# Batch 0's x in four loads in place of two, and the first states' cast ahead of alpha's turn

## The chip, the cores and the metric

The kernel runs on one core of one Trainium2 chip. The metric is the device time of one execution in microseconds. A core has five engines that run side by side, each through its own list of instructions: TensorE (PE in the profile, with its weight loads as PEld), VectorE (DVE), ScalarE (ACT), GpSimd (POOL) and SyncE (SP). Loads and stores are issued by an engine as instructions of its list, and move on the core's 16 DMA engines.

## The reference

Cross attention between 512 tokens and 32 states per head, both ways, and then a two-layer block on the rows that come out, with a PReLU between the layers:

```python
B, H, S, Ns, D = (8, 8, 512, 32, 64)
scores = scale * np.matmul(x, state.transpose(0, 1, 3, 2))
a = softmax(scores)                      # over the 32 states
xread = np.matmul(a, state)
scores2 = scale * np.matmul(state, x.transpose(0, 1, 3, 2))
a2 = softmax(scores2)                    # over the 512 tokens
sread = np.matmul(a2, x)
rows = np.concatenate([xread, sread], axis=2)   # heads side by side: [B * 544, 512]
h = rows @ w_in                          # d_ff = 2048
g = np.maximum(h, 0.0) + alpha * np.minimum(h, 0.0)
return g @ w_out
```

(The softmaxes are written out in the reference; the names here stand for them.)

## The kernel before

Everything is computed in f16 with f32 sums. The program is a long list of tokens, `ORDER`, and a table `steps` that gives the function for each token. The loop at its end calls them one after another, and each call appends its instructions to the lists of the engines. No scheduler moves anything: the order of the tokens is the order on every engine. A token `xt.0.1.0.3` is a call of the step `xt` with the arguments 0, 1, 0, 3; a letter at the end of some tokens names the engine that does a copy (a is ScalarE, v is VectorE, p is GpSimd).

The work goes by batches 0 to 7. For each, x is loaded and transposed, the scores of tokens against states are built, and the two softmaxes follow. The states are multiplied with w_in first (`m`, copied out by `mo`), so that the hidden layer of a batch is a product of softmax weights with these (`F` and `f`), followed by the PReLU (`N` on ScalarE, `G` on VectorE) and the second layer (`S`, `P`).

The steps around the change are all in the first lines of `ORDER`:

- `lx0` (`load_x0`) loads batch 0's x into the tile `xg_0` in two pieces: the even heads, then the odd ones. It is issued by GpSimd and turns f32 into f16 on the way. All the loads of x, `w_in` (`wi`, four pieces), `w_out` (`wo`) and the later states (`lst`) are issued by GpSimd too. The first 512 state rows (tile `st0_32`) are loaded by SyncE and alpha (`al32`) by ScalarE, ahead of the list.
- `id` builds the identity on GpSimd, which every transpose on TensorE needs as an operand. `ni` makes a negative identity from it on VectorE.
- `oma` turns alpha into 1 - alpha on VectorE (four 32x32 transposes and one operation). The PReLU reads it.
- `stc` casts the first states to f16 on VectorE. `stt` transposes them on TensorE (eight matmuls), `sto` copies them out on ScalarE.
- `Z.7.n` issues products of zeros on TensorE, n blocks of 128 columns in instructions of up to 512; nobody reads the result.
- `xt.b.j.g` transposes four heads of one parity g of batch b (j is one half of the tokens). `xo` copies them out. For batch 0 the even heads come first.
- `lx.1` loads batch 1's x in one piece, and `xt.1...` transposes it on TensorE.

Transfers that GpSimd issues signal on eight semaphores in turn. The ninth load takes the first's again, so it waits until that load has landed.

The program's list begins:

```python
lx0.0 lx0.1 id ni.v wi.0 oma lst stc Z.7.32 stt.2 sto.a lx.1 wi.1 dd.0.0.v wi.2 Z.7.3 xt.0.0.0.6
xo.0.0.0.v xt.0.1.0.3 xo.0.1.0.v Z.7.10 xt.0.0.1.4 xt.0.1.1.0 xo.0.1.1.v dd.0.1.a sd.0.0.5 hm.0.0
```

Of the kernel before, what the change touches and what calls it, by code (L numbers as in the profile page):

```python
# [14 lines left out]


ORDER = """
lx0.0 lx0.1 id ni.v wi.0 oma lst stc Z.7.32 stt.2 sto.a lx.1 wi.1 dd.0.0.v wi.2 Z.7.3 xt.0.0.0.6
xo.0.0.0.v xt.0.1.0.3 xo.0.1.0.v Z.7.10 xt.0.0.1.4 xt.0.1.1.0 xo.0.1.1.v dd.0.1.a sd.0.0.5 hm.0.0
xo.0.0.1.a sd.0.1.6 hm.0.1 sc.0.2.1.2 tm.0 hs.0.0 he.0.0 ssum.0.0 wi.3 Z.3.2 hs.0.1 he.0.1 ssum.0.1  # L20
m.1.0.7.4 mo.1.0.a.1.0 m.0.0.3.0 mo.0.0.a.1.1 tms.0 mo.0.0.a.0 str.0.5 sro.0.a str.1.6 sro.1.v
# [118 lines left out]
def kernel(  # L140
# [56 lines left out]
    xgs = {}  # L197
# [16 lines left out]
    nc.scalar.dma_start(al32[:n_jc, :], moe_alpha.rearrange("(jc p) -> jc p", p=128))  # L214
    xgs[0] = att.tile([128, H, 2, 2, D], F16, name="xg_0", tag="xg", bufs=4)

    def load_x0(g):
        nc.gpsimd.dma_start(  # L218
            xgs[0][:, g::2].rearrange("p k j r d -> p k (j r d)"),
            x[0, g::2].rearrange("k (p j r) d -> p k (j r d)", j=2, r=2),  # L220
        )

    osb_all = consts.tile([128, 4, d_model], F32)
# [583 lines left out]
    def product_sum(b, i, n):  # L807
# [16 lines left out]
        "m": state_w_in, "mo": state_w_in_out,  # L824
        "F": first, "f": first_part, "Z": zeros, "N": negative, "G": prelu, "S": second, "O": second_out,
        "st": stored, "lx0": load_x0, "lf": load_x0_32, "cx": x0_cast, "id": identity,
        "L": second_piece, "LO": second_piece_out, "Ls": second_piece_stored,
        "W": weight_sum, "A": hidden_sum, "P": product, "C": product_out, "D": product_sum,
# [34 lines left out]
```

## Time and profile before

| what | value |
|---|---|
| runs of the kernel | 207.89, 208.69, 210.45 us; median 208.69 |
| profiled execution | 207.22 us |
| its span, first to last instruction | 205.4 us |
| granted TensorE clock | 1.00 throughout |
| HBM read, written | 17.31 MB, 8.91 MB |
| DMA queue of GpSimd's loads | 12704 packets, 8.59 MB |

The span is what the trace shows; 1.82 us of the profiled execution lie outside it. In the lines of the profile, L218 is line 218 of the kernel, `out<-in` are tiles by the program's names, x16 is a count of instructions, and what stands behind `<-` in brackets is what ended the engine's idle time ahead of the row. PE times overlap from one matmul to the next, since matmuls are pipelined. A DMA issue on POOL's list has the time that POOL spends on it; the landing is a time of its own.

### The profile page before, as it was taken

The numbers are of one execution on the slowest core, as the hardware profiler recorded it, in microseconds if no ns is written. First come the engines' busy times: TensorE is split into PE (matmuls) and PEld (weight loads), VectorE is DVE, ScalarE is ACT, GpSimd is POOL, SyncE is SP. The second block draws the span as 40 slices with busy tenths as digits, with TensorE's granted clock in tenths as the row PEclk, the third lists the DMA queues.
The fourth block names the chain that finished last, engine by engine and source line by source line (L and its number), as shares of the span: only waits on it lengthen the run. The fifth ranks groups of instructions, "written<-read, shape, count | busy, mean of one in ns | idle before, by whom it ended". The sixth has DMA issues, their size and how long they took to land.

```text
span 205.4 us, 5181 instructions
## 1 busy us (share of the span) xinstructions
PE 197.1 (96%) x2023; PEld 131.4 (64%) x2023; DVE 181.6 (88%) x321; ACT 145.2 (71%) x319; POOL 159.6 (78%) x136
## 2 busy tenths in 40 slices
PE   7887999999999999999999999999999999999993
PEld 2542344445757766766557776776778777788882
DVE  4799999999999989999899999989999699995841
ACT  2599997889897679899898878869666476411120
POOL 7575489999989979998998899987997988502220
PEclk9999999999999999999999999999999999999999
DMA  5999999995999342749990135022000220031124
GB/s 81 195 203 209 204 206 197 185 232 54 163 163 178 66 153 58 100 103 158 194 163 3 53 123 135 3 105 102 0 0 3 111 93 3 2 131 62 69 102 156
DMA packets 39257, 23.22 MB, mean 113 GB/s; under 512 B 22320, under 2 KB 35008, under 8 KB 39232
## 3 DMA queue, kind: packets, MB, share of 16 engines
q0 software_dynamic: 12704, 8.59, 29.3%
q1 hardware_dynamic: 26496, 14.29, 28.4%
q8 instruction: 16, 0.26, 0.6%
q14 instruction: 9, 0.07, 0.2%
q10 hardware_dynamic: 32, 0.01, 0.0%
HBM read 17.31 MB, written 8.91 MB: 128 GB/s over the span
## 4 chain that ended last, share of the span: by engine, by line
PE 85%; DVE 5%; DMA 5%; POOL 1%; ACT 1%; issue 1%; ACTq 0%; POOLq 0%
PE ps L793 44%; PE ps L620 24%; PE ps L675 7%; DMA xg<-in_x_dram 5%; PE ps L629 3%; PE ps L590 3%; DVE gt_all L656 3%; PE ps L553 1%; ACT neg_all L652 1%; PE ps L362 1%; DVE m_all L603 1%; POOL xg L218 1%; DVE ts L466 1%; DVE nb L514 1%; DVE mx L476 1%
## 5 line engine op out<-in xcount | busy, mean ns | idle before, releaser
L656 DVE SCALAR_TENSOR_TENSOR gt_all<-neg_all,oma_sb,ps 128x512 f16<-128x512 f32 x128 | 89.3, 738 | 3.0 <-ACT neg_all L652 2.7
L652 ACT ACTIVATE neg_all<-ps 128x512 f32<-128x512 f32 (+1 forms) x144 | 77.4, 598 | 20.0 <-PE ps L620 14.4
L620 PE MATMUL ps<-aT,m_all 128*128 128x512 f16 x250 | 66.4, 379 | 0.3 <-DVE m_all L603 0.2
L765 POOL TENSOR_TENSOR hc_all<-gt_all 128x512 f16<-128x512 f16 x43 | 49.2, 1160 | 11.4 <-DVE osb_all L810 8.7
L793 PEld LDWEIGHTS <-hc_all 128*128 128x128 f16 x480 | 46.3, 98 | 14.3 <-issue 1.1
L793 PE MATMUL ps<-wc,hc_all 128*128 128x256 f16 x360 | 47.7, 273 | 0.0
L793 PEld LDWEIGHTS <-gt_all 128*128 128x128 f16 x336 | 32.6, 98 | 8.3 <-issue 0.5
L805 ACT COPY osb_all<-ps 128x256 f32<-128x256 f32 x51 | 19.1, 383 | 25.7 <-PE ps L793 22.2
L620 PEld LDWEIGHTS <-m_all 128*128 128x128 f16 x250 | 24.0, 98 | 18.0 <-issue 2.2
L603 ACT CAST m_all<-ps 128x512 f16<-128x512 f32 x58 | 31.6, 621 | 4.3 <-PE ps L590 4.3
L765 POOL TENSOR_TENSOR hc_all<-gt_all,hc_all 128x512 f16<-128x512 f16 x22 | 25.4, 1164 | 6.3 <-DVE hc_all L765 6.1
L793 PE MATMUL ps<-w_out_sb,gt_all 128*128 128x256 f16 x224 | 29.7, 273 | 0.0
L765 POOL TENSOR_TENSOR hc_all<-hc_all,gt_all 128x512 f16<-128x512 f16 x21 | 24.3, 1164 | 3.9 <-DVE hc_all L765 3.6
L810 DVE TENSOR_TENSOR osb_all<-osb_all,ps 128x256 f32<-128x256 f32 x45 | 18.0, 413 | 7.6 <-PE ps L793 4.7
L496 POOL TENSOR_TENSOR an<-ts,r 128x1024 f16<-128x1024 f32 (+1 forms) x9 | 15.5, 1725 | 6.2 <-DVE r L493 4.0
L482 POOL TENSOR_TENSOR ts<-ts,mx 128x1024 f32<-128x1024 f32 x7 | 13.4, 1918 | 5.4 <-DVE mx L476 5.4
L675 PE MATMUL ps<-w_out_sb,gt_all 128*128 128x512 f16 x64 | 16.6, 380 | 0.1
L793 PE MATMUL ps<-w_out_sb,hc_all 128*128 128x256 f16 x120 | 16.5, 273 | 0.0
L793 PE MATMUL ps<-wc,gt_all 128*128 128x256 f16 x112 | 14.7, 273 | 0.0
L590 PE MATMUL ps<-w_in_sb,stT 64*32 64x512 f16 x256 | 11.8, 383 | 1.9 <-DMA w_in_sb<-in_moe_w_in_dram 0.9
L527 ACT ACTIVATE e<-ps,nb 128x512 f16<-128x512 f32 x16 | 11.1, 705 | 0.1
L675 PEld LDWEIGHTS <-gt_all 128*128 128x128 f16 x64 | 5.9, 98 | 7.2 <-issue 1.2
(78 smaller groups left out, 204.6 us busy)
## 6 DMA issues: line engine op xcount, KB each, us to landing
out_dram<-osb_all SPq DMA_DIRECT2D x33, 256.0 KB, 2.6
xg<-in_x_dram POOLq DMA_DIRECT2D x7, 512.0 KB, 9.1
w_in_sb<-in_moe_w_in_dram POOLq DMA_DIRECT2D x4, 512.0 KB, 12.0
w_out_sb<-in_moe_w_out_dram POOLq DMA_DIRECT2D x4, 512.0 KB, 13.6
xg<-in_x_dram POOLq DMA_DIRECT2D x2, 256.0 KB, 4.5
out_dram<-osb_all SPq DMA_DIRECT2D x2, 128.0 KB, 2.4
gs_all<-in_state_dram POOLq DMA_DIRECT2D x1, 192.0 KB, 6.8
st<-in_state_dram SPq DMA_DIRECT2D x1, 128.0 KB, 2.4
```

The source lines that it names most:

```text
L482: engine(e).tensor_tensor(ts, ts, over_blocks(cols(softmax_tile("mx", b), j, S // N)), ALU.subtract)
L496: engine(e).tensor_tensor(blocks(cols(softmax_tile("an", b), j, S)), blocks(cols(softmax_tile("ts", b), j, S)), over_blocks(cols(softmax_t ...
L590: nc.tensor.matmul(banks[N * k : N * (k + 1), (k0, k1)[g], :], st_head(b, 2 * k + g)[64 * g : 64 * g + 64, :], w_in_sb[64 * g : 64 * g + 6 ...
L603: copier(e)(ms[b, f][:, g, :], banks[:, live["mp", b, f][g], :])
L620: nc.tensor.matmul(h.rearrange("p (r t) -> p r t", r=2), ms[b, f][:, g, 128 * j : 128 * (j + 1)], weights(b, g), start=(g == 0), stop=(g = ...
L652: nc.scalar.activation(neg, h, RELU, bias=0.0, scale=-1.0)
L656: nc.vector.scalar_tensor_tensor(gts[b, f][:, j, :], negs.pop((b, jc)), oma_sb[:, jc : jc + 1], hs.pop((b, jc)), ALU.mult, ALU.add,)
L675: nc.tensor.matmul(outs[b, q], hidden(b, jc, q), w_out_sb[:, jc, :], start=(jc == 0), stop=(jc == n_jc - 1),)
L765: engine(e).tensor_tensor(t, x, y, ALU.add if s == 1 else ALU.subtract)
L793: nc.tensor.matmul(outs[b, i, bank], rows, cols, start=(p in (1, 2, 5) and jc == 0), stop=(jc == n_jc // 2 - 1), skip_group_check=True,)
L805: copier(e)(rows_at(b, q, k)[:, 256 * half : 256 * (half + 1)], outs[b, i, "x"])
L810: nc.vector.tensor_tensor(to, to, outs[b, i, bank], ALU.add)
```

## The change

Batch 0's x comes in four loads of two heads each: heads 0 and 2, 4 and 6, 1 and 3, 5 and 7. The first states' cast moves from behind alpha's step to just behind the identity's token, ahead of the negative identity and of alpha. The first zero products are 28 blocks (seven instructions of 512 columns) in place of 32 (eight).

```diff
-lx0.0 lx0.1 id ni.v wi.0 oma lst stc Z.7.32 stt.2 sto.a lx.1 wi.1 dd.0.0.v wi.2 Z.7.3 xt.0.0.0.6
+lx0.0.0 lx0.0.1 lx0.1.0 lx0.1.1 id stc ni.v wi.0 oma lst Z.7.28 stt.2 sto.a lx.1 wi.1 dd.0.0.v wi.2 Z.7.3 xt.0.0.0.6
...
-    def load_x0(g):
+    def load_x0(g, i):
+        pair = slice(4 * i + g, 4 * i + g + 3, 2)
         nc.gpsimd.dma_start(
-            xgs[0][:, g::2].rearrange("p k j r d -> p k (j r d)"),
-            x[0, g::2].rearrange("k (p j r) d -> p k (j r d)", j=2, r=2),
+            xgs[0][:, pair].rearrange("p k j r d -> p k (j r d)"),
+            x[0, pair].rearrange("k (p j r) d -> p k (j r d)", j=2, r=2),
         )
```

On GpSimd, the start of the list, before the change (xg_75 is batch 0's x, xg_124 batch 1's, gs_all holds the later states, DMASW0 to 7 are the eight semaphores of its loads):

```order
L218 DMA xg_75<-in_x_dram 128x4x256 x2
masks.py:197 MEMSET ident 128x128
masks.py:199 ISA
masks.py:199 AFFINE_SELECT ident<-ident 128x128 [waits Pool_49]
L253 DMA w_in_sb<-in_moe_w_in_dram 128x4x512
L247 DMA gs_all<-in_state_dram 128x768
L201 DMA xg_124<-in_x_dram 128x8x256
L253 DMA w_in_sb<-in_moe_w_in_dram 128x4x512 x3
```

And the same place now, where lines from 218 on stand one further down and batch 1's x is xg_125:

```order
L219 DMA xg_75<-in_x_dram 128x2x256 x4
masks.py:197 MEMSET ident 128x128
masks.py:199 ISA
masks.py:199 AFFINE_SELECT ident<-ident 128x128 [waits Pool_49]
L254 DMA w_in_sb<-in_moe_w_in_dram 128x4x512
L248 DMA gs_all<-in_state_dram 128x768
L201 DMA xg_125<-in_x_dram 128x8x256
L254 DMA w_in_sb<-in_moe_w_in_dram 128x4x512
L254 DMA w_in_sb<-in_moe_w_in_dram 128x4x512 [waits DMASW0_49]
L254 DMA w_in_sb<-in_moe_w_in_dram 128x4x512 [waits DMASW1_49]
```

Four issues stand ahead of the identity in place of two, and the third and fourth piece of w_in wait for the first and the second load of x. Each w_out piece, and each later batch of x, waits for the same load as before, by another semaphore, save the first two w_out pieces, which wait for the third and the fourth load of x.

On VectorE, the start of the list, before (al_72 is alpha, st_32_70 the first states in f32, gs_all holds their f16 copy and the negative identity):

```order
L394 MEMSET gs_all 128x256 x2
L384 TENSOR_SCALAR gs_all<-ident 128x128 [waits Pool_49]
L305 STREAM_TRANSPOSE alT<-al_72 32x32 [waits DMAHW1_49,DVE_49]
L305 STREAM_TRANSPOSE alT<-al_72 32x32 x3
L306 TENSOR_SCALAR oma_sb<-alT 128x16 [waits DVE_49]
L292 CAST gs_all<-st_32_70 128x256 [waits DMAHW0_49]
L398 COPY gs_all<-ps 64x8x32 [waits Activation_49]
```

And now:

```order
L395 MEMSET gs_all 128x256 x2
L293 CAST gs_all<-st_32_70 128x256 [waits DMAHW0_49]
L385 TENSOR_SCALAR gs_all<-ident 128x128 [waits Pool_49]
L306 STREAM_TRANSPOSE alT<-al_72 32x32 [waits DMAHW1_49,DVE_49]
L306 STREAM_TRANSPOSE alT<-al_72 32x32 x3
L307 TENSOR_SCALAR oma_sb<-alT 128x16 [waits DVE_49]
L399 COPY gs_all<-ps 64x8x32 [waits Activation_49]
```

The cast of the first states stands ahead of the operation that waits for GpSimd's identity, and waits only for its own load; alpha's five instructions stand behind both. On TensorE one zero product is gone ahead of the first states' transposes, and within the transposes of the even heads the first two now wait for the first load and the third for the second; the odd heads' wait for the third and the fourth load in the same way. ScalarE's and SyncE's lists are unchanged.

## The prediction

> **What bounds the kernel now.** I read the page's busy shares first, then the busy time by stretch, to see where the busiest engine is not busy.
>
> ```profile
> PE 197.1 (96%) x2023; PEld 131.4 (64%) x2023; DVE 181.6 (88%) x321; ACT 145.2 (71%) x319; POOL 159.6 (78%) x136
> ```
> ```profile
> 0.00:25.00 25.00, 20.45 (x283) 8.95 (x284) 20.08 (x40) 17.81 (x39) 15.36 (x23) 1.00 1.14 178
> 25.00:200.00 175.00, 174.75 (x1733) 120.99 (x1726) 160.63 (x281) 127.01 (x281) 144.24 (x114) 1.00 0.51 103
> ```
>
> The columns of the second view are the stretch and its length, then busy time of PE, PEld, DVE, ACT and POOL, the granted clock, the DMA share and GB/s. From 25 to 200 us TensorE is idle for 0.25 us; in the first 25 us it is idle for 4.55 us, and the DMA engines move 178 GB/s. The change edits only the program's first steps. So it can act in one way: by how much earlier or later TensorE's unbroken work begins. The ceiling is a few microseconds of 207.22.
>
> The chain of waits in order of time says what sets that beginning.
>
> ```profile
> 1.25 0.47 POOL xg L218
> 3.52 0.71 POOL w_in_sb L253
> 4.23 0.53 POOL gs_all L247
> 4.76 9.53 DMA xg<-in_x_dram
> 14.29 0.05 issue
> 14.34 1.07 PE ps L340 x16
> 15.41 0.45 PE ps L641 x2
> 25.12 1.89 PE ps L675 x8
> ```
>
> (Start, length, what; rows between some of these are left out.) One DMA, the load of batch 1's x, holds 9.53 us of the head. It is issued at 4.76 and lands at 14.29, and batch 1's sixteen transposes start at 14.34. Nothing on the chain before it is arithmetic; it is POOL issuing loads in order. The question is therefore what the change does to that landing, and what would be late next if it came sooner.
>
> **The loads on POOL's queue.** POOL issues every load of the head in order, and its identity lies between them:
>
> ```profile
> 1.25 1.69 POOL L218 DMA_DIRECT2D xg<-in_x_dram  x2 [0.80 <-POOLq L847]
> 3.22 0.29 POOL masks.py:199 TENSOR_SCALAR_AFFINE_SELECT ident<-ident 128x128 f16<-128x128 f16 x1
> 3.46 0.77 POOL L253 DMA_DIRECT2D w_in_sb<-in_moe_w_in_dram  x1
> 4.23 0.55 POOL L247 DMA_DIRECT2D gs_all<-in_state_dram  x1
> 4.76 0.91 POOL L201 DMA_DIRECT2D xg<-in_x_dram  x1
> 5.65 2.26 POOL L253 DMA_DIRECT2D w_in_sb<-in_moe_w_in_dram  x3
> ```
> ```profile
> L218 POOL DMA_DIRECT2D xg<-in_x_dram x2: 748/844/941, 1.2 to 2.2; - x2
> DMA to landing us min/median/max: 4.3/4.5/4.7
> ```
>
> The state load has 128 rows and takes 0.55 us to issue, a load of four heads (128x4 rows) 0.75 when it is not the first (the minimum above), a whole batch (128x8 rows) 0.91. The trace has no load of 256 rows. On the line between 128 and 512 rows it costs 0.55 + 0.20 x 128/384 = 0.62. The first load of all took 0.94, so 0.19 more; I keep that once. Now: 0.94 + 0.75 = 1.69. After: 4 x 0.62 + 0.19 = 2.67, which is **0.98 us more on POOL**. The bounds are four at the state load's price, 2.39 (0.70 more), and four at 0.75, 3.19 (1.50 more). I take 0.98, since the rows lie on both sides of it.
>
> Everything behind moves by that: the identity from 3.51 (3.22 + 0.29) to 4.49, the issue of w_in's first piece from 3.46 to 4.44, the states, batch 1's x to 5.74. Two of the later w_in issues now wait for the first and the second of the four loads; those land before 5.6 (below) and the issues come after 7, so these waits cost nothing.
>
> **Does a later issue mean a later landing?** Only if the queue runs dry. The DMA rates of the head:
>
> ```profile
> 3.00:3.25 0.25, 0.25 (x2) 0.15 (x1) 0.00 (x0) 0.00 (x0) 0.17 (x2) 1.00 0.44 10
> 3.25:3.50 0.25, 0.25 (x2) 0.07 (x1) 0.00 (x0) 0.00 (x0) 0.25 (x2) 1.00 0.03 4
> 3.50:3.75 0.25, 0.25 (x2) 0.08 (x1) 0.20 (x2) 0.00 (x0) 0.25 (x2) 1.00 0.39 39
> 3.75:4.00 0.25, 0.25 (x2) 0.14 (x1) 0.24 (x2) 0.00 (x0) 0.25 (x1) 1.00 1.23 150
> 4.00:5.00 1.00, 0.95 (x5) 0.04 (x5) 0.85 (x5) 0.00 (x0) 1.00 (x3) 1.00 1.44 196
> 5.00:6.00 1.00, 1.00 (x16) 0.83 (x17) 0.00 (x0) 0.41 (x1) 1.00 (x2) 1.00 1.46 197
> ```
>
> The last number is GB/s. Few bytes move before 3.5; the stream then holds 196 to 197. Batch 0's x is 2 x 256 KB (524,000 bytes written). Up to 6.00 the rows give 0.25 x (39 + 150) + 196 + 197 = 440,000, so the rest is through at about 6.43. The whole head is this one stream: batch 1's x lands when everything queued before it has gone through. Two things can move it.
>
> Its start: the first issue ends at 1.25 + 0.94 = 2.19 now, and at 1.25 + 0.62 + 0.19 = 2.06 after, so **0.13 us earlier**. The bounds are nothing (the stream starts by something else), and 0.25 earlier if it hangs on the second issue's end (2.94 now, 2.68 after).
>
> Its supply: w_in's issue ends at 4.23 now and at 5.21 after. The first load's bytes were seen from 3.00 on, 0.81 us after its issue ended, and the full stream from about 3.76 (the point from which 196 GB/s would give the same bytes), 1.57 after. With 0.81, w_in is ready at 6.02 and batch 0's x is through at 6.43 - 0.13 = 6.30: no gap. With 1.57 it is ready at 6.78: a gap of 0.48. I take no gap, because the slow stretch between 3.0 and 3.5 is that of an idle queue, and this queue is not idle; but the margin is 0.28 us, so the gap stays as a rival.
>
> A fixed price of each further load in the stream: the two loads are issued at 1.25 and 2.18 (1.25 + 0.94) and land 4.3 and 4.7 us later, at 5.55 and 6.88. That is 1.33 apart, which is 262,000 bytes at 197 GB/s. So I take nothing. [...]
>
> **The first states and the zero product.** TensorE's and VectorE's rows:
>
> ```profile
> 1.32 3.60 PE L272 MATMUL ps<-gs_all 128*128 128x512 f16 x8 [1.32 <-DVE gs_all L266]
> 2.15 0.15 PEld L272 LDWEIGHTS <-gs_all 128*128 128x128 f16 x1 [0.28 <-issue]
> 2.58 0.15 PEld L272 LDWEIGHTS <-gs_all 128*128 128x128 f16 x1 [0.28 <-issue]
> 4.96 0.58 PE L286 MATMUL ps<-ident,gs_all 128*64 128x128 f16 x8
> 5.65 0.61 PE L340 MATMUL ps<-ident,xg 128*128 128x128 f16 x8
> 6.93 0.62 PE L340 MATMUL ps<-ident,xg 128*128 128x128 f16 x8
> 15.24 0.59 PE L641 MATMUL ps<-aT,m_all 128*128 128x512 f16 x2
> ```
> ```profile
> 1.27 0.55 DVE L394 MEMSET gs_all<- 128x256 uint32 x2
> 3.66 0.84 DVE L305 STREAM_TRANSPOSE alT<-al 32x32 f32<-32x32 f32 x4
> 4.62 0.29 DVE L292 CAST gs_all<-st 128x256 f16<-128x256 f32 x1
> 13.45 1.30 DVE L504 STREAM_TRANSPOSE aT<-an 128x512 f16<-128x512 f16 x2
> 16.51 1.41 DVE L656 SCALAR_TENSOR_TENSOR gt_all<-neg_all,oma_sb,ps 128x512 f16<-128x512 f32 x2 [0.15 <-ACT neg_all L652]
> ```
>
> Eight zero products of 0.43 us (2.15 to 2.58) end at 4.92, the cast at 4.91, and the first states' transposes start at 4.96. With seven products TensorE is free at 4.49; the cast, moved ahead of alpha, is done well before; the identity comes at 4.49. So they start at about 4.54, 0.42 earlier (at POOL's upper bound, identity at 5.01, 0.10 later). That 0.42 has no buyer: the transposes of x behind them would start at 5.23 in place of 5.65, but their second load lands at 5.55 - 0.13 = 5.42. They wait. The same holds for the second half, which starts at 6.93 because its load lands at 6.88: now two of its transposes run on the third load, and six remain when the fourth lands at 6.75, so batch 0 is some 0.25 us earlier there. That too is hidden: batch 0's weights are ready at 14.75 (13.45 + 1.30) and their second product runs at about 15.45, so this branch already has 0.7 us to spare against batch 1's x. Alpha moves later by about 1 us, and its first reader is at 16.51.
>
> The cast now falls beside POOL's fourth issue. POOL's first issue, beside VectorE's fill of 0.55 us, took 0.94; the second, beside nothing, 0.75. [...] The row against it is batch 1's issue at 4.76, which ran beside the end of the cast at 4.62 and took 0.91, the least that any of the seven whole-batch issues took:
>
> ```profile
> L201 POOL DMA_DIRECT2D xg<-in_x_dram x7: 914/922/944, 4.8 to 90.0; - x7
> ```
>
> I take nothing for it.
>
> **The sum.** Batch 1's x lands at 14.29 - 0.13 = 14.16, w_in's pieces in the same stream move alike, and the end moves with them: 207.22 - 0.13 = 207.09 by the profiled execution, whose span of 205.4 leaves 1.82 outside. The runs shown are 207.89, 208.69 and 210.45; with the profiled one the middle of the four is 208.29, and less 0.13 that is **208.2**.
>
> **Rivals.**
>
> - *The stream runs dry ahead of w_in* (slower). It decides from the point where the four issues take over 0.28 us more than I sum, or where bytes follow an issue as late as they did the first, 1.57 us. Price: a gap of 0.48 less 0.13, so 0.35 later; at the upper bound of POOL's cost 0.52 more, 0.87. Time 208.6 to 209.2. For it: the margin is small. Against: the queue is not idle. Chance 0.27.
> - *The slow start shrinks* (faster). If the 0.5 us of few bytes (3.0 to 3.5) depends on the first load's size, the stream starts up to 0.5 earlier; w_in's issue then comes late and takes some of it back. Gain 0.4: 207.9. Chance 0.12.
> - *TensorE's clock rises later*. Its products cost 0.43 us per 512 columns at first a quarter of that, 0.11, per 128; eight of batch 0's x transposes then take 0.61 where that rate would make at least 0.86, so a faster rate arrives before 5.65. A pause after seven products could put it off; batch 0's branch would lose about 1 us of products, less its 0.7 to spare and the 0.25 gained: 0 to 0.3 later. Chance 0.06.
> - *Each load pays alone in the stream*. A load's landing comes 4.3 us after its issue starts, of which 1.33 is bytes: 3.0 us each, two more loads, 214.1. The 1.33 between two landings speaks against it. Chance 0.02.
>
> **Chances and range.** The forecast itself, from 0.25 earlier to 0.2 later, has 0.51; 0.02 is left on either side for what I don't see. About 2%, or 4.2 us, is what a measurement of this kernel can tell from no change. Only the single-payment case and what is left reach beyond it: faster 0.02, slower 0.04, within 0.94. The range is the rivals' ends set on the runs' scatter: from 207.22 - 0.4 = 206.8 to 208.69 + 0.87 = 209.6.
>
> **What would show it.** Right: POOL's four issues take about 2.7 us, the identity ends near 4.5, the first states' transposes start at 4.5 to 4.6, TensorE then waits for the second load until about 5.4, the fourth lands near 6.75, and batch 1's transposes start near 14.2, again released by the DMA. Wrong: a DMA rate well below 190 between 6 and 7 us and a landing of batch 1's x after 14.5 (the dry stream); zero products still at 0.43 us after 6 us (the clock); or batch 1's transposes released by anything but the load, which would mean that the chain was never the stream's.

## The result and the profile after

The changed kernel takes 211.22 us (median of six runs, 209.79 to 212.18) against 208.64 for the kernel before (six runs, 207.89 to 210.45): a ratio of 1.0138, with a 95% interval of 1.0100 to 1.0176. It is slower by 1.4%, some 2.6 us, where 0.13 less was forecast. That is under the 2% that one measurement was said to tell, but the interval is clear of 1, and a second set of runs below repeats it.

The profiled execution of the changed kernel took 209.79 us, its span 208.0, at a granted clock of 1.000; before, 207.22 and 205.4. So the two traces, too, differ by 2.6 us. Busy time by stretch, the changed kernel (columns as in the prediction: stretch, length, PE, PEld, DVE, ACT, POOL, clock, DMA share, GB/s):

```profile
0.00:25.00 25.00, 18.15 (x268) 8.21 (x269) 19.26 (x38) 16.16 (x35) 15.65 (x25) 1.00 1.09 165
25.00:200.00 175.00, 174.36 (x1717) 119.32 (x1716) 161.06 (x280) 128.02 (x282) 145.36 (x114) 1.00 0.53 103
```

From 25 to 200 us TensorE is nearly as full as before (0.64 us idle, before 0.25). In the first 25 us it is idle for 6.85 us, before for 4.55. The zero product of 0.43 us that it no longer has is a part of that; by the shifts below, 1.96 of the 2.6 us are lost there. The same stretch moved 165 GB/s, before 178, which points at the supply. The chain of waits of the changed kernel, its head (start, length, what):

```profile
1.25 1.33 POOL xg L219 x2
...
2.84 1.43 POOL xg L219 x2
...
4.87 0.72 POOL w_in_sb L254
5.59 0.55 POOL gs_all L248
6.13 0.90 POOL xg L201
7.03 1.45 POOL w_in_sb L254 x2
8.48 15.88 DMA w_in_sb<-in_moe_w_in_dram
24.36 0.04 issue
24.40 0.41 PE ps L591 x8
```

The DMA that holds the head is another one in this profile. Before, it was batch 1's x, landing at 14.29; now it is the last piece of w_in, landing at 24.36. (A second profile of the changed kernel, e8 below, has batch 1's x again.) All of it is still POOL issuing loads in order, and those issues show where the delay starts. POOL's list, the changed kernel:

```profile
1.25 3.03 POOL L219 DMA_DIRECT2D xg<-in_x_dram  x4 [0.80 <-POOLq L848]
4.57 0.29 POOL masks.py:199 TENSOR_SCALAR_AFFINE_SELECT ident<-ident 128x128 f16<-128x128 f16 x1
4.81 0.78 POOL L254 DMA_DIRECT2D w_in_sb<-in_moe_w_in_dram  x1
6.12 0.91 POOL L201 DMA_DIRECT2D xg<-in_x_dram  x1
```

The four loads by their line, with the duration of an issue (min, median, max), and the time from an issue's start to its landing:

```profile
L219 POOL DMA_DIRECT2D xg<-in_x_dram x4: 719/722/885, 1.2 to 3.6; - x4
DMA to landing us min/median/max: 3.3/4.1/4.2
```

A load of 256 rows takes 0.72 us to issue, not 0.62. Half the rows save 0.03 of the 0.75 that a load of 512 took, so two more loads cost POOL 3.03 - 1.69 = 1.34 us. The first piece of w_in is issued 1.35 us later than before (4.81 against 3.46), batch 1's x 1.36 later.

The DMA rates of the changed kernel, to be set against the prediction's rows of before:

```profile
3.00:3.50 0.50, 0.50 (x3) 0.22 (x2) 0.29 (x1) 0.00 (x0) 0.50 (x1) 1.00 0.75 65
3.50:4.00 0.50, 0.50 (x3) 0.08 (x1) 0.00 (x0) 0.00 (x0) 0.50 (x2) 1.00 1.35 181
4.00:5.00 1.00, 0.57 (x5) 0.21 (x5) 0.10 (x1) 0.00 (x0) 0.93 (x4) 1.00 1.18 144
5.00:6.00 1.00, 0.71 (x11) 0.38 (x10) 0.93 (x7) 0.59 (x1) 1.00 (x2) 1.00 1.25 158
6.00:6.50 0.50, 0.14 (x3) 0.14 (x4) 0.27 (x2) 0.20 (x1) 0.50 (x2) 1.00 1.20 152
6.50:7.00 0.50, 0.50 (x8) 0.38 (x7) 0.32 (x1) 0.17 (x1) 0.50 (x2) 1.00 0.82 52
7.00:7.50 0.50, 0.50 (x5) 0.22 (x3) 0.44 (x2) 0.00 (x0) 0.50 (x2) 1.00 0.55 69
7.50:8.00 0.50, 0.34 (x7) 0.33 (x6) 0.00 (x0) 0.00 (x0) 0.50 (x2) 1.00 1.18 176
```

Bytes start earlier and rise faster, as the second rival had it. Then, up to 8 us, the stream never reaches the 196 to 197 GB/s of before: it runs at 144 to 158 from 4.0 to 6.5, while the small loads pass, falls to 52 and 69 between 6.5 and 7.5, and comes back after that. One issue of 128 KB every 0.72 us would make 182 GB/s, so the pace of the issues alone does not explain 144 to 158. For comparison, before:

```profile
6.00:7.00 1.00, 0.87 (x9) 0.36 (x7) 0.80 (x3) 0.54 (x2) 1.00 (x2) 1.00 1.31 175
7.00:8.00 1.00, 0.90 (x40) 0.68 (x40) 0.56 (x3) 0.59 (x1) 0.91 (x2) 1.00 1.24 199
```

What TensorE makes of that in the changed kernel (the bracket is its idle time ahead of the row, and what ended it):

```profile
4.92 0.41 PE L287 MATMUL ps<-ident,gs_all 128*64 128x128 f16 x8 [0.43 <-POOL ident masks.py:199]
5.44 0.28 PE L341 MATMUL ps<-ident,xg 128*128 128x128 f16 x2
6.36 0.51 PE L341 MATMUL ps<-ident,xg 128*128 128x128 f16 x6 [0.65 <-DMA xg<-in_x_dram]
...
7.68 0.51 PE L341 MATMUL ps<-ident,xg 128*128 128x128 f16 x6 [0.15 <-DMA xg<-in_x_dram]
...
11.07 0.63 PE L591 MATMUL ps<-w_in_sb,stT 64*32 64x512 f16 x16 [0.73 <-DMA w_in_sb<-in_moe_w_in_dram]
...
15.40 1.07 PE L341 MATMUL ps<-ident,xg 128*128 128x128 f16 x16 [0.59 <-DMA xg<-in_x_dram]
...
24.40 0.41 PE L591 MATMUL ps<-w_in_sb,stT 64*32 64x512 f16 x8 [0.83 <-DMA w_in_sb<-in_moe_w_in_dram]
```

And the row of before that answers to the last of these:

```profile
22.44 0.41 PE L590 MATMUL ps<-w_in_sb,stT 64*32 64x512 f16 x8
```

Matching TensorE's instructions of the two traces one by one gives the shift along the head: 0.60 later at 6.36, 0.94 at 11.07, 1.06 at 15.40 and 1.96 at 24.40, each time behind a wait for a DMA. Two short waits later, at 77 and 122 us, bring it to 2.58. The last step of the head is worth a look: before, that product began at 22.44 without a wait, and w_in's last piece had landed at 22.40. A product that does wait starts as long after its landing (24.40 after 24.36), so this load had no slack that the trace can tell. The chain of waits of before could not show that, since it names only what came last.

The landings, worked out from the trace's records (us; the pieces of batch 0's x in the order of issue):

| load | before | after |
|---|---|---|
| batch 0's x | 5.58, 6.89 | 4.50, 6.32, 6.97, 7.63 |
| w_in, first piece | 10.09 | 11.03 |
| batch 1's x | 14.29 | 15.35 |
| w_in, pieces 2, 3, 4 | 16.72, 19.25, 22.40 | 17.90, 20.48, 24.36 |

### The profile page after: what moved, and what is told of

The parts are those of the page before. It is cut to its first block, busy times and chain, and to the rows that moved or that the text cites. A ratio compares the mean times of both kernels' runs of the same rounds, so it can differ in the third digit from the quotient of the medians.

```text
span 208.0 us, 5181 instructions
## 1 busy us (share of the span) xinstructions
PE 197.0 (95%) x2022; PEld 131.3 (63%) x2022; DVE 182.1 (88%) x321; ACT 145.3 (70%) x319; POOL 161.0 (77%) x138
## 3 DMA queue, kind: packets, MB, share of 16 engines
q1 hardware_dynamic: 26496, 14.29, 28.8%
## 4 chain that ended last, share of the span: by engine, by line
PE 72%; DMA 14%; DVE 6%; POOL 3%; ACT 2%; issue 1%; ACTq 0%; DVEq 0%; POOLq 0%
PE ps L794 37%; PE ps L621 21%; DMA w_in_sb<-in_moe_w_in_dram 8%; PE ps L676 7%; DMA out_dram<-osb_all 6%; PE ps L630 3%; DVE gt_all L657 3%; PE ps L591 3%; POOL xg L219 1%; POOL w_in_sb L254 1%; DVE osb_all L811 1%; ACT neg_all L653 1%; PE ps L554 1%; DVE nb L515 1%; DVE r L493 1%
## 5 line engine op out<-in xcount | busy, mean ns | idle before, releaser
(78 smaller groups left out, 205.4 us busy)
```

## The experiments

The first four tell the change's parts apart. Three theories were written down for them: *Supply* (POOL's longer issues let the queue of loads run dry), *Small loads* (each split load is slow in itself), and *Cast* (the moved cast and the missing zero product do the harm). The diffs are of the first line of the list against before, unless said otherwise.

**e1: the four loads alone**, cast and zero products as before.

```diff
-lx0.0 lx0.1 id ni.v wi.0 oma lst stc Z.7.32 stt.2 sto.a lx.1 wi.1 dd.0.0.v wi.2 Z.7.3 xt.0.0.0.6
+lx0.0.0 lx0.0.1 lx0.1.0 lx0.1.1 id ni.v wi.0 oma lst stc Z.7.32 stt.2 sto.a lx.1 wi.1 dd.0.0.v wi.2 Z.7.3 xt.0.0.0.6
```

> Only the four loads; the cast and the eight zero products stand as before. Supply (POOL reaches w_in's first piece 1.35 us later and the DMA queue runs dry): w_in's first piece lands near 11.0 in place of 10.1, time 2 to 3 us above before. Small loads (the two-head transfers themselves are slow): the same, 2 to 3 us above. Cast (the order on VectorE and the missing zero product cost it): within 0.8 us of before.

210.88 us against 208.44: 1.0119 (1.0057 to 1.0182). The loads alone make the loss. Its rates, again per stretch, show the same hole:

```profile
5.00:6.00 1.00, 0.00 (x0) 0.00 (x0) 0.93 (x7) 0.00 (x0) 1.00 (x2) 1.00 1.29 155
6.00:7.00 1.00, 0.67 (x9) 0.50 (x10) 0.28 (x2) 0.00 (x0) 1.00 (x2) 1.00 1.15 99
7.00:8.00 1.00, 1.00 (x9) 0.83 (x10) 0.37 (x2) 0.64 (x2) 1.00 (x3) 1.00 0.80 78
```

w_in's last piece lands at 24.17. Without the moved cast the first states' transposes wait for VectorE behind alpha, since the identity is late:

```profile
6.33 0.64 PE L287 MATMUL ps<-ident,gs_all 128*64 128x128 f16 x8 [1.42 <-DVE gs_all L293]
```

In the changed kernel they start at 4.92. So the cast does what it was moved for: it saves 1.41 us at that place. In e1's profile the chain of waits names no DMA: it goes through the identity, alpha's steps, the cast and the transposes of batch 0's x, which end at 10.07. The total hardly shows it (1.0119 against 1.0138, intervals over one another).

**e2: the cast and the seven zero products alone**, two loads as before.

```diff
-lx0.0 lx0.1 id ni.v wi.0 oma lst stc Z.7.32 stt.2 sto.a lx.1 wi.1 dd.0.0.v wi.2 Z.7.3 xt.0.0.0.6
+lx0.0 lx0.1 id stc ni.v wi.0 oma lst Z.7.28 stt.2 sto.a lx.1 wi.1 dd.0.0.v wi.2 Z.7.3 xt.0.0.0.6
```

> Only the cast ahead of alpha and seven zero products; x in two loads. Supply and small loads: within 0.5 us of before, w_in's first piece lands at 10.0 to 10.2, batch 1's x near 14.3. Cast: 2 to 3 us above before, or at least batch 0's transposes later than 6.93 at the second half.

209.22 us, 1.0034 (1.0000 to 1.0068). A third of a per cent: not the cause of 1.4%. Its profile does show the sign that was set for *Cast*, batch 0's x transposed late, since its loads landed at 7.01 and 8.34. The runs of e7 and e11 decide that.

**e3: the delay without the split.** Two fills of a part of `m_all` that is used only later stand on POOL between the identity and w_in's first issue, which they move from 3.46 to 4.60. The fills are extra work; nothing reads them.

```diff
-lx0.0 lx0.1 id ni.v wi.0 oma lst stc Z.7.32 stt.2 sto.a lx.1 wi.1 dd.0.0.v wi.2 Z.7.3 xt.0.0.0.6
+lx0.0 lx0.1 id ni.v pz wi.0 oma lst stc Z.7.32 stt.2 sto.a lx.1 wi.1 dd.0.0.v wi.2 Z.7.3 xt.0.0.0.6
...
+    def pause():
+        nc.gpsimd.memset(m_all[:, 13], 0.0)
+        nc.gpsimd.memset(m_all[:, 12, 0, :256], 0.0)
```

> Before with two GpSimd fills of unused memory, about 1.4 us, between the identity and the issue of w_in's first piece; x in two loads that keep their times. Supply: batch 0's x lands at 5.6 and 6.9 as before, the queue is dry for about 1 us, w_in's first piece lands at 10.9 to 11.2, batch 1's x at 15.1 to 15.4, time 1.2 to 2.6 us above before. Small loads: the queue is not dry or it does not matter, w_in's first piece at 10.1 to 10.4, time within 0.5 us of before.

209.18 us, 1.0033 (0.9993 to 1.0074). w_in's first piece lands at 10.25, its last at 22.51: a stall of the stream (130 GB/s between 6 and 7 us), but *Supply* had forecast 10.9 to 11.2 for the first piece and 1.2 to 2.6 us of time; the time is 0.7 us more than before, with an interval that holds 1. So 1.14 us of delay at w_in's issue is not enough for the loss.

**e4: three loads**, the even heads in one, the odd ones in two.

```diff
-lx0.0.0 lx0.0.1 lx0.1.0 lx0.1.1 id stc ni.v wi.0 oma lst Z.7.28 stt.2 sto.a lx.1 wi.1 dd.0.0.v wi.2 Z.7.3 xt.0.0.0.6
+lx0.0 lx0.1.0 lx0.1.1 id ni.v wi.0 oma lst stc Z.7.32 stt.2 sto.a lx.1 wi.1 dd.0.0.v wi.2 Z.7.3 xt.0.0.0.6
...
-        pair = slice(4 * i + g, 4 * i + g + 3, 2)
+        pair = slice(g, None, 2) if i is None else slice(4 * i + g, 4 * i + g + 3, 2)
```

(against the changed kernel)

> Even heads in one load, odd heads in two. Supply: three issues at about 0.72 to 0.9 each, w_in's first issue at 4.1 to 4.2 in place of 3.46, a gap of 0.2 to 0.5 us in the queue, w_in's first piece lands at 10.2 to 10.6, time 0.3 to 1.2 us above before. Small loads: half of the whole, 1.3 to 1.5 us above before, with the odd heads landing 0.4 us late or more. If each further issue simply adds its length to the end: 0.7 us above.

208.84 us, 1.0027 (0.9992 to 1.0062). The loads of two heads land at 6.62 and 7.29, 0.68 and 0.67 us behind the load ahead of each: 128 KB at 196 GB/s. A load of two heads is not slow when a bigger one stands ahead of it in the queue, and w_in's last piece lands at 21.85. *Small loads* falls for that case, and *Supply* needs a finer form.

The second set asks which part of the supply it is. *Shallow queue*: split loads pass one at a time through an empty queue. *Issue delay*: only the later issue of everything behind matters. *Clock*, a supposition that no trace had shown: TensorE's idle time in the head lets its clock drop.

**e5: the delay by two more issues, without the split.** Two loads of four bytes per row (256 rows each, into a part of `m_all` that is used only later, read by nobody) stand behind the two big ones.

```diff
-lx0.0 lx0.1 id ni.v wi.0 oma lst stc Z.7.32 stt.2 sto.a lx.1 wi.1 dd.0.0.v wi.2 Z.7.3 xt.0.0.0.6
+lx0.0 lx0.1 dm.0 dm.1 id ni.v wi.0 oma lst stc Z.7.32 stt.2 sto.a lx.1 wi.1 dd.0.0.v wi.2 Z.7.3 xt.0.0.0.6
...
+    def tiny_load(i):
+        nc.gpsimd.dma_start(
+            m_all[:, 12 + i, :, :2], x[0, 0:2, 0:128, 0:2].rearrange("k p d -> p k d")
+        )
```

> x in its two loads; behind them two loads of 256 rows of 4 bytes into memory that is written later, so that GpSimd issues four loads ahead of the identity and w_in's first issue comes at 4.7 to 4.9 as with the change, but nothing is split. Shallow queue (an issue costs about 0.72 us whatever its rows, a two-head load is 0.67 us of bytes, so split loads never build a lead): x lands at 5.6 and 6.9, w_in's first piece at 10.3 to 10.6, its last at 23.0 or earlier, time 0.3 to 1.0 us above before. Issue delay (only the lateness of w_in's issue counts, split or not): w_in's first piece at 10.9 or later, its last at 23.8 or later, time 2 to 3 us above before. Clock (TensorE's pause ahead of the first states puts off its faster clock): the pause is 1.4 us here as in the run with the four loads alone, so 2 to 3 us above before, with the stream as before.

209.0 us against 208.12: 1.0048 (1.0004 to 1.0092). POOL issues w_in's first piece at 4.86 here, at 4.81 in the changed kernel, and batch 1's x lands even later (15.73 against 15.35); yet the loss is a third. The difference stands in the rates:

```profile
5.00:6.00 1.00, 0.00 (x0) 0.00 (x0) 0.93 (x6) 0.00 (x0) 1.00 (x2) 1.00 1.45 196
6.00:6.50 0.50, 0.13 (x4) 0.13 (x6) 0.31 (x2) 0.00 (x0) 0.50 (x2) 1.00 2.07 155
6.50:7.00 0.50, 0.50 (x11) 0.34 (x10) 0.00 (x0) 0.17 (x1) 0.50 (x1) 1.00 1.52 39
7.00:7.50 0.50, 0.50 (x10) 0.43 (x8) 0.06 (x1) 0.41 (x1) 0.50 (x2) 1.00 0.75 111
7.50:8.00 0.50, 0.50 (x6) 0.32 (x5) 0.50 (x3) 0.24 (x1) 0.50 (x2) 1.00 1.24 207
```

196 GB/s up to 6 us, a hole between 6.5 and 7.5, and full again. Up to 7.0 the DMA engines are at the rows of four bytes as well (DMA share 2.07 and 1.52; these two loads land at 7.10 and 7.26), so only a part of the hole is a dry queue. Together they cost the first w_in piece 0.35 us (10.44 against 10.09) and the last one 0.72 (23.12).

**e6: w_in first behind the split loads**, ahead of the identity, so that it is issued at 4.26 in place of 4.81. Against the changed kernel:

```diff
-lx0.0.0 lx0.0.1 lx0.1.0 lx0.1.1 id stc ni.v wi.0 oma lst Z.7.28 stt.2 sto.a lx.1 wi.1 dd.0.0.v wi.2 Z.7.3 xt.0.0.0.6
+lx0.0.0 lx0.0.1 lx0.1.0 lx0.1.1 wi.0 id stc ni.v oma lst Z.7.28 stt.2 sto.a lx.1 wi.1 dd.0.0.v wi.2 Z.7.3 xt.0.0.0.6
```

> The change, with w_in's first piece issued straight behind the four loads and the identity behind it. Shallow queue and issue delay: w_in's first issue at 4.28 in place of 4.81, it lands at 10.4 to 10.7 in place of 11.0, its last piece 0.4 to 0.6 us earlier than with the change, time 0.4 to 0.6 us below the change. Clock: the identity comes at 5.6, TensorE pauses 1.1 us ahead of the first states, time no better than the change, or worse by up to 1 us.

210.96 us, 1.0120 (1.0039 to 1.0200). Nothing comes back that four runs can tell. *Shallow queue* and *Issue delay* had both forecast 0.4 to 0.6 us less than the change, and missed; only *Clock* had forecast no gain. With no pause on POOL between the four loads and w_in, the stream is slow all the same, and for longer:

```profile
4.00:5.00 1.00, 0.41 (x2) 0.11 (x1) 0.00 (x0) 0.00 (x0) 1.00 (x2) 1.00 1.33 175
5.00:6.00 1.00, 0.31 (x8) 0.25 (x7) 0.31 (x3) 0.00 (x0) 0.93 (x4) 1.00 1.27 145
6.00:7.00 1.00, 1.00 (x15) 0.76 (x12) 0.94 (x6) 0.59 (x1) 1.00 (x2) 1.00 1.02 104
7.00:8.00 1.00, 0.65 (x5) 0.11 (x2) 0.70 (x4) 0.37 (x1) 1.00 (x3) 1.00 1.28 141
8.00:9.00 1.00, 0.86 (x38) 0.64 (x38) 0.39 (x1) 0.58 (x1) 1.00 (x2) 1.00 0.96 154
```

w_in's first piece, issued 0.55 us earlier than in the changed kernel, lands at 12.55, 1.52 later, held up by three of its sixteen parts (see the landings below); its last piece lands at 23.87, 0.49 earlier, as both had forecast. *Issue delay* falls as the whole cause, and *Shallow queue* does not say why the stream is slow for so long.

**e7 and e11: the cast alone**, with all eight zero products; e11 is the same kernel in a second set of more rounds.

```diff
-lx0.0 lx0.1 id ni.v wi.0 oma lst stc Z.7.32 stt.2 sto.a lx.1 wi.1 dd.0.0.v wi.2 Z.7.3 xt.0.0.0.6
+lx0.0 lx0.1 id stc ni.v wi.0 oma lst Z.7.32 stt.2 sto.a lx.1 wi.1 dd.0.0.v wi.2 Z.7.3 xt.0.0.0.6
```

> Only the cast ahead of alpha; x in two loads and the eight zero products as before, so TensorE has no pause between zero products and states. Clock: within 0.3 us of before, where the run with seven products was 0.8 above. Shallow queue and issue delay say nothing of the products: the same as the run with seven, 0 to 0.8 us above before.

> The cast ahead of alpha alone, with eight zero products and two loads, once more and in more rounds, since it was the fastest so far. If it gains: 0.2 to 0.5 us below before, by the first states leaving TensorE a little sooner and no pause. If that was scatter: within 0.2 us of before.

207.72 us, 0.9984 (0.9950 to 1.0019), and 208.35 us, 0.9988 (0.9953 to 1.0023). The moved cast costs nothing; a gain of a tenth of a per cent may be there, but both intervals hold 1. *Clock* had forecast no loss for e7, the other two the 0 to 0.8 us of e2. The eighth zero product, which e2 lacks and e7 has, may be worth the half per cent between them, but their intervals overlap. It does not explain the change: e1 and e12 have all eight and lose as much.

**e8: the changed kernel once more.** No edit.

> The changed kernel once more. Shallow queue: 2 to 3 us above before; batch 0's x lands at 7.5 to 7.8, w_in's first piece at 10.9 to 11.9, its last after 23.8; the DMA rate between 6.5 and 7.5 is under half of the full rate. Clock: the time goes with the moment at which TensorE's products become fast, and a run in which that is early is within 1 us of before.

210.79 us, 1.0116 (1.0064 to 1.0169): the loss repeats. Its rates have the hole too (76 and 78 GB/s in the two halves of 6.5 to 7.5), and w_in's last piece lands at 23.96. That piece does not hold TensorE here: the chain of waits goes through batch 1's x, which lands at 16.34, and the product that reads the piece starts 1.37 us after it landed.

```profile
6.13 10.21 DMA xg<-in_x_dram
...
25.33 0.63 PE L591 MATMUL ps<-w_in_sb,stT 64*32 64x512 f16 x8
```

**e12: TensorE kept busy in the pauses**, as a test of *Clock*: the changed kernel with 32 blocks of zeros again, and 12 in place of 3 behind the states' transposes. Against the changed kernel:

```diff
-lx0.0.0 lx0.0.1 lx0.1.0 lx0.1.1 id stc ni.v wi.0 oma lst Z.7.28 stt.2 sto.a lx.1 wi.1 dd.0.0.v wi.2 Z.7.3 xt.0.0.0.6
+lx0.0.0 lx0.0.1 lx0.1.0 lx0.1.1 id stc ni.v wi.0 oma lst Z.7.32 stt.2 sto.a lx.1 wi.1 dd.0.0.v wi.2 Z.7.12 xt.0.0.0.6
```

> The change with eight zero products again ahead of the states, and twelve blocks in place of three behind them, so that TensorE does not pause ahead of batch 0's x. Clock (the pauses put off or take back its faster clock): 0.5 us or more below the change, ratio to before 1.008 or less. Shallow queue: as the change, ratio 1.010 to 1.014, w_in's last piece after 23.8.

211.70 us, 1.0152 (1.0092 to 1.0212). No gain, so *Clock* is not borne out in that form; the DMA is still what TensorE waits for, and longer than in the changed kernel:

```profile
13.04 0.64 PE L591 MATMUL ps<-w_in_sb,stT 64*32 64x512 f16 x16 [2.53 <-DMA w_in_sb<-in_moe_w_in_dram]
```

**e9 and e10: a deep queue ahead of the split loads.** w_in's first piece goes ahead of batch 0's x, with x in two loads (e9, against before) and in four (e10, against the changed kernel).

```diff
-lx0.0 lx0.1 id ni.v wi.0 oma lst stc Z.7.32 stt.2 sto.a lx.1 wi.1 dd.0.0.v wi.2 Z.7.3 xt.0.0.0.6
+wi.0 lx0.0 lx0.1 id ni.v oma lst stc Z.7.32 stt.2 sto.a lx.1 wi.1 dd.0.0.v wi.2 Z.7.3 xt.0.0.0.6
...
-lx0.0.0 lx0.0.1 lx0.1.0 lx0.1.1 id stc ni.v wi.0 oma lst Z.7.28 stt.2 sto.a lx.1 wi.1 dd.0.0.v wi.2 Z.7.3 xt.0.0.0.6
+wi.0 lx0.0.0 lx0.0.1 lx0.1.0 lx0.1.1 id ni.v oma lst stc Z.7.32 stt.2 sto.a lx.1 wi.1 dd.0.0.v wi.2 Z.7.3 xt.0.0.0.6
```

> w_in's first piece issued ahead of everything, x in two loads behind it: the pair to the next run. Both theories: w_in's first piece lands near 7.0, x at about 8.3 and 9.6, and batch 0 is some 2.5 us later than before; time 1 to 3 us above before.

> The same with x in four loads, so that the split loads stand behind 2.6 us of bytes in the queue. Shallow queue (split loads cost only where nothing is queued ahead of them): the four land 0.65 to 0.75 us apart, the last within 0.3 us of the run with two, w_in's last piece within 0.3 us, time within 0.6 us of it. Small loads (two-head loads are slow wherever they stand): the last lands 0.7 us or more later than there, time 1.5 us or more above it.

211.58 us, 1.0147 (1.0088 to 1.0206), and 211.55, 1.0140 (1.0090 to 1.0189). In both, batch 0's x comes later than before (9.85 and 10.45 in place of 6.89), and both are slower than before. By the medians, split and whole loads now give the same time. At a full granted clock four loads are slower: e9's two such runs took 210.66 and 210.93, e10's four 211.29 to 211.73. The four loads of e10 by their line:

```profile
L219 POOL DMA_DIRECT2D xg<-in_x_dram x4: 704/708/717, 2.2 to 4.3; - x4
DMA to landing us min/median/max: 6.1/6.2/6.2
```

All four land 6.1 to 6.2 us after their issue: evenly behind one another, with the queue full. w_in's last piece lands at 21.87, with two loads at 21.96. The pair bears out *Shallow queue* in the main: from the landing of w_in's first piece (7.14 in e9, 7.66 in e10) to x's last load it takes 2.71 us with two loads and 2.79 with four, though these are issued at the same pace (0.71 us each) as at the head. So behind 512 KB the split itself costs the stream next to nothing. The forecast that x's last load would land within 0.3 us of e9's missed: it is 0.60 later, 0.52 of it in w_in's piece ahead of any split load, and no run tells why. In both kernels TensorE waits for batch 0's x, so a smaller price on w_in could not be seen in the time.

What singles out the split loads at the head is seen best in the landings of batch 0's four loads (us, from the trace's records):

| kernel | landings | steps between them |
|---|---|---|
| after | 4.50, 6.32, 6.97, 7.63 | **1.82**, 0.65, 0.66 |
| e1 | 4.66, 5.45, 6.12, 7.73 | 0.79, 0.67, **1.61** |
| e6 | 4.64, 5.30, 7.32, 8.02 | 0.66, **2.02**, 0.70 |
| e8 | 4.67, 5.71, 7.25, 7.92 | 1.04, **1.54**, 0.67 |
| e12 | 4.66, 5.32, 7.14, 7.81 | 0.66, **1.82**, 0.67 |
| e10, behind w_in | 8.38, 9.02, 9.70, 10.45 | 0.64, 0.68, 0.75 |

A step of 0.67 is the bytes alone. In the profile of every one of the five kernels with four loads at the head, one step is 1.5 to 2.0 us long, at no fixed place; behind the deep queue none is. And w_in's last piece lands between 23.87 and 24.36 in these five profiles, between 21.85 and 23.12 in all the others.

The records behind a landing say what a long step is. The trace has sixteen reports of arrival for each load, and the landing is the last of them. Of the changed kernel's second load fifteen reports come between 4.86 and 5.34, and the sixteenth at 6.32. By the middle of the sixteen its four loads arrive at 4.34, 5.07, 6.05 and 6.76, in steps of 0.70 to 0.98. So the long step there is one straggler among sixteen parts, and not a load that is slow as a whole; in e6 four parts are late, in e12 six. Stragglers are not the split's alone: in e7, with two loads, fifteen reports of w_in's first piece come by 9.38 and the last at 11.46.

The stream as a whole is late too. By the middle of its reports w_in's last piece arrives between 21.91 and 23.09 in the five, at 20.68 before, and between 20.59 and 21.72 in all the others. The two latest of those have the delay without the split: e3 with 21.51 and e5 with 21.72. So the delay makes a good part of the lateness, and the split adds to it.

**The clock.** The runs also differ in the granted clock. In some of them it drops to half for a stretch; e8's profile has one (columns as above):

```profile
20.00:23.30 3.30, 2.00 (x27) 0.48 (x26) 3.30 (x4) 3.30 (x9) 0.04 (x1) 1.00 1.25 209
23.40:26.70 3.30, 3.16 (x14) 0.80 (x14) 3.13 (x5) 2.48 (x6) 1.41 (x1) 0.50 1.24 205
27.00:30.00 3.00, 3.00 (x22) 1.17 (x20) 2.43 (x5) 3.00 (x7) 3.00 (x3) 1.00 1.24 206
```

A run whose mean clock is under 0.996 takes about 1.4 us longer (before: 209.50 against 208.06 in the first set of runs). Such runs were 16 of 22 among the kernels with four loads at the head (the changed one, e1, e6, e8, e12), and 19 of 60 of the kernel before. Taken apart by that clock, the four-load kernels average 210.0 against 208.1 for before at full clock, and 211.5 against 209.5 under it. So at equal clock the loss is 1.9 us, and the larger share of lowered runs makes the rest, 0.41 x 1.4 = 0.6. That the pauses bring the lower clock is not shown: e12 filled two of them and had it in all four of its runs.

## Why the prediction was wrong

**The kernel's bound: right.** The change acted through the supply of the head, and the time beyond 25 us followed it.

**POOL's issues: mis-sized.** The line through 128 and 512 rows gave 0.62 for 256; the measured 0.72 makes four issues 3.03 us, not 2.67, inside the bounds given (+1.34, of +0.70 to +1.50). w_in's first issue ends at 5.59 in place of 5.21. e5's loads of four bytes per row, also 256 rows, took 0.70 and 0.73: the bytes don't matter, and between 256 and 512 rows hardly the rows. The 0.36 us more are past the 0.28 from which the prediction let its first rival decide.

**The supply: the step that failed.** The prediction took "no gap", with 0.81 us between an issue's end and its bytes. The time to a full stream counts instead. In the changed kernel and in e5 w_in's issue ends at 5.59 and 5.64, and the rows pass 170 GB/s from 7.5 on, 1.9 us later; in e3 it is 1.6 us (from 5.37 to 7.0), and in e1, e6 and e12 the rows from 7 to 9 us stay under 170. Before, 4.23 + 1.9 = 6.13 lay just ahead of the end of x's bytes at 6.43; after, 7.5 lies 1.2 us behind the forecast 6.30. Batch 1's x, forecast to land 0.13 us earlier, landed 1.06 later. The prediction's own sign of a dry stream came: 152 and 52 GB/s between 6 and 7 us, and that landing at 15.35. The rival of the dry stream was right as far as it went. Its price, 0.35 to 0.87, fits e5 (0.48% of 208.12 is 1.0 us, with the interval from 0.1 to 1.9) better than the change.

**"A fixed price of each further load: nothing." Wrong where it mattered.** It was read from two landings 1.33 us apart, of loads whose issues are 0.94 and 0.75 apart: the bytes of each took longer than the next issue. With two heads it is the other way round, 0.72 for the issue and 0.67 for the bytes. On this reading, the best that the runs allow, the queue never fills, and a load meets it empty or nearly so; e1's first three land 2.53, 2.61 and 2.56 us after their issues' ends. With 0.67 us of bytes in each, about 1.9 us of that stand beside the bytes, an estimate from these three; e10's four land in steps of 0.64 to 0.75, so there, behind 512 KB, it was not paid again for each load. In the changed kernel itself the first load lands 2.37 us after its issue's end and the others 3.35 to 3.47, so this price does not account for them alone. The rival that priced it for each load, 214.1, had the right ingredient without that condition, and was too dear.

**The gain of an earlier start: real, and lost at once.** The first load, with half the bytes, landed at 4.50, 1.08 us earlier than before, but its two transposes start at 5.44, behind the states', and the other six wait until 6.36.

**The states' branch: right.** The cast costs nothing beside POOL's issues (POOL's second to fourth issue took 0.72 each in the changed kernel, where the cast ran at 3.04 beside the third, and 0.72 to 0.73 in e1, with no cast beside them). Forecast to start at 4.54, the states' transposes start at 4.92, since the identity is late by POOL's longer issues. TensorE's products did not become fast later in the changed kernel's first profile: its eight transposes of states take 0.41 us at 4.92, before 0.58 at 4.96. In e8 they take 0.64 at 4.93, but in e12, with no pause ahead of them, 0.64 at 4.91 as well; that a pause puts the faster rate off, as the rival on the clock supposed, was not shown. The gain of the moved cast "has no buyer": e7 and e11 show none that clears their intervals.

**What would be late next: missed.** The prediction let w_in's pieces move "alike" and looked at batch 1's x for the end. The changed kernel's first profile has w_in's last piece 1.96 us later and TensorE waiting for it; that piece had nothing to spare before. Which load comes last is not fixed, though: in e8, the same kernel, it is batch 1's x at 16.34, and in e6 and e12 the later states at 13.50 and 13.95. Nor does the landing of x tell the time: e5 has it at 15.73, later than the changed kernel's first profile, and is some 0.8% faster (1.0048 against 1.0116 to 1.0138).

**A slip in the chances.** They add up to 1.02; nothing hangs on it.

**Left open.** Why the stream of the kernels with four loads is later than the delay alone makes it. In e6, where w_in stands right behind the split loads, the rate stays at 104 to 157 GB/s for four more microseconds. Single packets of 1.1 to 2.1 us appear in that trace between 6 and 8 us, but e2 and e7, with two loads, have packets of 1.2 to 1.3 us as well, and no run separates their cause. The changed kernel has a second dip between 11 and 14 us, 146 to 173 GB/s where there were 191 to 216 before, and that is not explained either. The long way of w_in's last piece from the third's landing, 3.88 us in the changed kernel against 2.53 in e8, is a straggler: by the middle of the reports it is 2.53 and 2.58. No version clearly beats the kernel before.

## What to carry to other kernels

Before a load is split, compare the issue of a piece with its bytes, and ask what stands ahead of it in the queue. Here 0.72 us of issue against 0.67 us of transfer was the wrong side by a hair, and the price at the head of the stream was not 0.05 us a piece but a stream that was late as a whole; behind 512 KB the same split cost the stream next to nothing (2.79 us against 2.71). When the binder of a chain is moved, look for what arrives second, by its slack: here it had none, and the chain of waits never named it. Take the time from an issue to a full stream, not to its first byte, when asking whether a queue runs dry (here 1.6 to 1.9 us). And look at the reports behind a landing before calling a load late: one part of sixteen can set it (fifteen by 5.34 us, the last at 6.32, for the changed kernel's second load).

## What the runs showed of the hardware

- An issue's time on POOL hardly depends on the bytes: 0.70 to 0.73 for 256 rows of four bytes, 0.72 for 256 rows of two heads, 0.75 for 512 rows. More rows do count over a wider span: 0.55 for 128, 0.91 for 1024.
- The clock at half lasted 3.41 us a time in two profiles (0.50 from 23.44 to 26.86 in e1 and from 23.35 to 26.76 in e8; 1.00 in the stretch of that length ahead of each). In e8 TensorE was busy for 2.00 of the 3.30 us from 20.00 to 23.30, just ahead of it. A stretch about as empty was not followed by a fall in the profile of before (2.11 of 3.42 us busy from 18.99, then 1.00), so what brings the fall is not shown.
- A fill on POOL held up a VectorE operation beside it, which I had not allowed for in e3. VectorE's step on the identity took 1.16 us there, until both fills were over, in place of 0.20; the first of alpha's transposes waited behind it, and the other three took 0.20 each as ever. The row of before, and e3's:

```profile
3.55 0.20 DVE L384 TENSOR_SCALAR gs_all<-ident 128x128 bf16<-128x128 f16 x1 [1.74 <-POOL ident masks.py:199]
```

```profile
3.54 1.16 DVE L384 TENSOR_SCALAR gs_all<-ident 128x128 bf16<-128x128 f16 x1 [1.73 <-POOL ident masks.py:199]
```

- Landings differ between runs with the same loads: batch 0's x landed at 5.58 and 6.89 in the profile of before, at 5.98 and 7.30 in e7's, and at 7.01 and 8.34 in e2's. The middle of the sixteen reports hardly does (5.45, 5.42 and 5.48 for the first load); one part was late in e7, four in e2.
